# Weight sums for a seven-product output projection: made earlier, in place, in buffers that are idle until the operands come

## The chip, the cores and the metric

One core of a Trainium2 chip runs the kernel. The metric is the time of one execution on the device, in microseconds. The kernel before takes 945.11 us (median of three runs, 944.76 to 945.55).

## What is computed

Sliding-window attention (window 64) is followed by two gated layers. With 4 x 576 = 2304 tokens:

```python
x = attention(q, k, v)                                   # (2304, 512)
x = (sigmoid(x @ w_gate) * (x @ w_val)) @ w_out          # inner width 1536
y = ((x @ w_a) * (x @ w_b)) @ w_out2                     # inner width 1536
```

The inputs q, k and v are float32, and the weights come as 64-bit words, which the kernel decodes into a high and a low float32 part on VectorE, ScalarE and GpSimd. Every product is taken as three matmuls (high x high, high x low, low x high) in the reduced-width float32 form of TensorE.

## The kernel before, in words

Tokens are in nine blocks of 256. Blocks 0 to 4 are the front, in groups (0), (1, 2), (3, 4). Blocks 5 to 8 are the back, whose attention is made meanwhile and parked in DRAM. The inner width is cut into 12 chunks of 128 per layer; chunks F = 0 to 11 are layer 1, and 12 to 23 layer 2.

*The ordered list.* The first ten turns of the plan, with the attention of the front, are an order written out by hand (`RAMP`, with `in_order()` behind it).

*The later turns.* Turns n = 10 to 18 follow: (0) with three chunks, (1, 2) x 3, (3, 4) x 3, (0) x 3, (1, 2) x 2, (3, 4) x 1, (3, 4) x 2, (1, 2) x 2, (0) x 2. A turn makes the gate and value products of its chunks (`hidden`, matmuls `gps` and `vps`, line 450), and the projection that it leaves in the queue is run in the next turn (`accm`, line 551, added into `gacc` on VectorE, line 528). Between the matmuls the loop calls a step of the weight decoder once or twice per block. In turns 10 to 13 (`SPAN`) it also moves the attention of the back along (scores `sps`, transposes `tps`, output `xps`). From turn 14 on the attention's buffers are closed, and pools for later work are opened in their place (`late`: `op6`, `hs`, `wq`, `sts`, `rs`).

*Who sets the order.* Behind the ordered list a planner in the framework places each instruction in the queue of its engine, by program order and by a simulated timeline; on the chip each engine runs its queue in order. A tile that reuses another one's buffer is planned behind all accesses of that other one, also behind those that come later in the program. `held_back(step)` ties what the step issues, in the planner's order alone, behind the newest TensorE instruction of the program (line 844). The chip knows no wait for that.

*The weight sums.* Chunks 0 to 9 of layer 1 are projected once more for the back, in five pairs (p = 0 to 4), by a seven-product scheme for 2 x 2 blocks (`seven`, line 949). It needs four sums of output-weight blocks per pair. `weight_sums(p)` (line 315) makes them in turns 14 to 18, and what is left behind turn 18. It loads the decoded weights from DRAM (for chunks under 7 as a high and a low part that GpSimd adds, line 329), makes four sums of 128x256 on GpSimd (line 338), splits each into high and low on ScalarE and VectorE (lines 340 and 341), and stores all to DRAM (`kept_sums`, line 343). A step makes all of the arithmetic of a pair at once, and the loop calls a step per block, unless layer-2 sums are under way (`combined_by`). Its buffers are from the `late` pools: `hs`, `rs`, `sts`, and `op6`, which has one buffer.

*The operands.* Behind turn 17, `front_operands` (line 715) begins to build the seven operands of the front's layer 2 from the results `b11, b21, b12, b22` (`gacc`). `high(nm, f)` copies f on ScalarE into the high half (line 730), `low(nm)` makes the low half on VectorE (line 736), and `minus(a, b)` puts a - b into b's place on VectorE (line 739). Operands 1 and 5 are placed in four quarters of a buffer set that nothing has used until then, and 6 is placed in `op6`:

```python
o = tuple(quarter(nm // 5, k, f"op{nm}") for k in range(2))     # op1: quarters (0, 0), (0, 1); op5: (1, 0), (1, 1)
for nm, f in ((1, b11), (2, b21)): high(nm, f); low(nm)
yield got                                                       # here turn 18 is put into the program
minus(b12, b11); high(5, b11); low(5); minus(b22, b12); minus(b22, b11); high(6, b11); low(6)
```

The layer-2 products of the front (`quad`, matmuls `qa`, `qb`, `qc` of line 861) use the operands in the order 1, 5, 6, 2, 7, 4, 3.

Of the kernel before, what the change touches and what calls it, by code (L numbers as in the profile page):

```python
# [10 lines left out]
F32 = mybir.dt.float32  # L11
F32R = mybir.dt.float32r
I32 = mybir.dt.int32
U32 = mybir.dt.uint32
AF = mybir.ActivationFunctionType
ALU = mybir.AluOpType
# [5 lines left out]
def tile_window_attention_gated_mlps(ctx, tc, q, k, v, w1g, w1v, w1o, w2a, w2b, w2o, out):  # L22
    nc = tc.nc
    B, H, S, D = q.shape
    NT, DM = out.shape
    DFF = w1g.shape[1]
    P = 128
# [7 lines left out]
    W = 2 * N  # L35
    CH = 2 * P
# [41 lines left out]
    for e in range(2):  # L78
        rows = slice(e * WIN, (e + 1) * WIN)
        nc.gpsimd.affine_select(  # L80
            out=mask_n[rows], in_=mask_n[rows], pattern=[[1, P]], compare_op=ALU.is_ge,
# [3 lines left out]
            out=mask_n[rows], in_=mask_n[rows], pattern=[[-1, P]], compare_op=ALU.is_ge,  # L85
# [159 lines left out]
    x, done = {}, set()  # L245
# [15 lines left out]
    def quarter(i, j, nm):  # L261
        return xs.tile([P, 2, W], F32R, tag=f"q{i}{j}", name=f"{nm}{i}{j}")
# [51 lines left out]

    def weight_sums(p):

        both = late["hs"].tile([P, 2, DM], F32R, tag="hs", name="of").bitcast(F32)
        lows = {}
        for i in range(2):
            F = 2 * p + i  # L320
            if F < DECODED:
                lows[i] = late["rs"].tile([P, W], F32, tag="r", name="ol")
                for j, t in enumerate((both[:, i], lows[i])):
                    nc.sync.dma_start(out=t, in_=kept[F, "o"][:, j])
            else:
                nc.sync.dma_start(out=both[:, i], in_=kept_o[F])
        yield
        for i, low in lows.items():
            nc.gpsimd.tensor_tensor(out=both[:, i], in0=both[:, i], in1=low, op=ALU.add)
        (a11, a21), (a12, a22) = ((both[:, i, 0:CH], both[:, i, CH:]) for i in range(2))  # L330
        u, v = (late["sts"].tile([P, CH], F32, tag="s", name="osum") for _ in range(2))
        o = late["op6"].tile([P, 4, 2, CH], F32R, tag="op6", name="opair")
        for todo in (
            ((u, a21, a22, ALU.add, 0), (v, a11, a21, ALU.subtract, 2)),
            ((u, u, a11, ALU.subtract, 1), (v, a12, u, ALU.subtract, 3)),
        ):
            for s, x, y, op, _ in todo:
                nc.gpsimd.tensor_tensor(out=s, in0=x, in1=y, op=op)
            for s, _, _, _, n in todo:
                nc.scalar.activation(out=o[:, n, 0], in_=s, func=AF.Copy)  # L340
                nc.vector.tensor_tensor(out=o[:, n, 1], in0=s, in1=o[:, n, 0].bitcast(F32), op=ALU.subtract)
        yield
        nc.sync.dma_start(out=kept_sums[p], in_=o.bitcast(F32))

    def load_matrix(F, nm):
        ph, fc = divmod(F, NF)
# [281 lines left out]
    begun, combined_by = [0], []  # L628
# [37 lines left out]
    def step_sums():  # L666

        if summing and 2 * summing[0][0] + 1 in ready and next(summing[0][1], summing) is summing:
            summing.pop(0)
            step_sums()  # L670
# [34 lines left out]
    late = {}  # L705
# [138 lines left out]
    def held_back(step):  # L844

        made = nc.cur_bb.bb.instructions
        since = len(made)
        at = next(i.name for i in reversed(made) if i.engine == mybir.EngineType.PE)
        step()
        for i in nc.cur_bb.bb.instructions[since:]:  # L850
            for after in (at, *copied[-1:]):
                tc.add_manual_dep(
                    i, after, mybir.DependencyInfo(mybir.DependencyClass.NoSync, mybir.DependencyReason.DATA), reason="held"
                )
# [94 lines left out]
    def seven(res, begin, o, sums, b):  # L949


        half = lambda w, i: tuple(p[:, i * CH:(i + 1) * CH] for p in w)
        at = lambda i: tuple(sums[i // 2][:, i % 2, p] for p in range(2))
        a = {1: half(o[0], 0), 2: half(o[1], 0), 3: at(3), 4: half(o[1], 1), 5: at(0), 6: at(1), 7: at(2)}
        jobs = []
        for c in range(2):
            sl, bank, written = slice(c * P, (c + 1) * P), {}, set()

            def job(n, k, start, dsts, bank=bank, sl=sl, c=c, written=written):
                if k not in bank:  # L960
                    bank[k] = ps_acc.tile([P, W], F32, tag="acc", name=f"acc{k}")
                for m, (i, j) in enumerate(((0, 0), (0, 1), (1, 0))):
                    nc.tensor.matmul(  # L963
                        bank[k], lhsT=a[n][i][:, sl], rhs=b[n][j], start=start and m == 0, stop=m == 2,
                        skip_group_check=True,
                    )
                for d in dsts:
                    dst = res[d][:, c]
                    if begin and d not in written:
                        nc.scalar.activation(out=dst, in_=bank[k], func=AF.Copy)  # L970
                    else:
                        nc.vector.tensor_tensor(out=dst, in0=bank[k], in1=dst, op=ALU.add)
                    written.add(d)

            for args in (
                (1, "x", True, (0,)), (2, "y", True, (0,)), (6, "x", False, (1,)), (5, "y", True, (3,)),
                (7, "x", False, (2, 3)), (3, "y", False, (1,)), (4, "y", True, (2,)),
            ):
                jobs.append(lambda args=args, job=job: job(*args))
        return jobs  # L980
# [99 lines left out]
    for n, (group, fcs) in enumerate(plan):  # L1080
        begin, end = fcs[0] == 0, fcs[-1] == NF - 1
        if n < len(FIRST):
            continue
        if n == SPAN.start:
            attend(FRONT[-1][-1])
            feed = attention_stream(BACK[BEHIND:])
        if n == SPAN.stop:
            attend(BACK[-1])
            attend(steps=100)
            next_part(early, (("op6", 1), ("hs", 1), ("wq", 8), ("sts", 4), ("rs", 3)), middle)  # L1090
            limit[0] = NF + 1
        hs = []
        for i, fc in enumerate(fcs):
            need(fc, n)
            hs.append((ready[fc], hidden(0, ready[fc], x[0, group])))
            for _ in range(-(-len(queue) // (len(fcs) - i))):
                queue.pop(0)()
            for _ in group:
                for _ in range(2 if late else 1):
                    step_decode(n)  # L1100
                if late and not combined_by:
                    step_sums()
                if n in SPAN:
                    due += STEPS / ticks
                    attend(steps=int(due))
                    due -= int(due)
        queue.append(lambda a=(group_of[group[0]], group, hs, begin, end): [(m(), e()) for m, e in first_projection(*a)])
        if n == len(plan) - 2:
            built = front_operands(FRONT[2], FRONT[1])
            x_ops = next(built)  # L1110
# [305 lines left out]
```

## Time and profile before

| what | value |
|---|---|
| the time shown: median of three runs | 945.11 us |
| the profiled execution: its time | 945.28 us |
| the profiled execution: first to last instruction | 943.5 us |
| TensorE busy | 922.2 us, 98% |
| VectorE busy | 706.6 us, 75% |
| ScalarE busy | 482.2 us, 51% |
| GpSimd busy | 306.9 us, 33% |

The profile is of one execution. PE is TensorE's matmuls, DVE is VectorE, ACT is ScalarE, POOL is GpSimd, and SP issues the DMAs. Matmuls are pipelined, so a busy PE is not a PE at its peak; what counts here is the time in which PE has no matmul at all, and who released it then.

### The profile page before, as it was taken

How to read it: one execution, taken by the hardware profiler on the slowest of the kernel's cores; microseconds unless marked ns; L12 is line 12 of the kernel's file. 1: busy time of each engine (PE TensorE's matmuls, PEld its weight loads, DVE VectorE, ACT ScalarE, POOL GpSimd, SP SyncE). 2: the span in 40 equal slices, each digit the busy share in tenths (PEclk: the TensorE clock that was granted, in tenths of full speed). 3: DMA queues.
4: the chain of work that ended last, by engine and by line, in shares of the span. 5: the costliest groups of instructions: out<-in, count | busy, mean ns of one | idle time of the engine just before them, and what ended most of it. 6: DMA issues, size and time to landing. Idle time of an engine off the chain costs nothing. (4 is left out here: it accounts for less than half of the span.)

```text
span 943.5 us, 15633 instructions
## 1 busy us (share of the span) xinstructions
PE 922.2 (98%) x5498; PEld 771.9 (82%) x5498; DVE 706.6 (75%) x1370; ACT 482.2 (51%) x1071; POOL 306.9 (33%) x325
## 2 busy tenths in 40 slices
PE   7899999999999999999999999999999999999998
PEld 6798888887888778878787787888888888888886
DVE  6997787786569799898999877687877773354455
ACT  7897555686644456664555446555444233211111
POOL 4543222343226714561655337354351000000000
PEclk9999999999999999999999999999999999999999
DMA  9988598988479626673767758555547675544212
GB/s 225 244 214 239 198 323 290 346 274 250 143 226 315 233 113 200 237 247 142 267 223 250 278 175 234 197 182 168 176 124 240 197 277 147 167 157 146 86 60 89
DMA packets 145566, 195.79 MB, mean 208 GB/s; under 512 B 63569, under 2 KB 98641, under 8 KB 144849
## 3 DMA queue, kind: packets, MB, share of 16 engines
q1 hardware_dynamic: 144400, 192.71, 63.0%
q0 software_dynamic: 1088, 2.10, 1.3%
q8 instruction: 43, 0.70, 0.3%
q14 instruction: 35, 0.28, 0.1%
HBM read 118.75 MB, written 71.57 MB: 202 GB/s over the span
## 5 line engine op out<-in xcount | busy, mean ns | idle before, releaser
L861 PE MATMUL qa<-op,wq 128*128 128x512 f32 x432 | 112.3, 390 | 1.8 <-ACT r L880 1.4
L861 PE MATMUL qb<-op,wq 128*128 128x512 f32 x432 | 111.1, 390 | 0.9 <-POOL wq L430 0.6
L880 ACT ACTIVATE r<-qa 128x512 f32<-128x512 f32 x108 | 62.9, 595 | 95.0 <-PE qa L861 93.4
L450 PE MATMUL gps<-xh,wa 128*128 128x256 f32 (+1 forms) x392 | 104.9, 338 | 1.1 <-DVE g L884 1.1
L450 PE MATMUL vps<-xh,wb 128*128 128x256 f32 (+1 forms) x392 | 105.4, 337 | 0.0
L861 PEld LDWEIGHTS qa<-op,wq 128*128 128x128 f32 x432 | 80.8, 188 | 19.4 <-ACT r L880 2.0
L861 PEld LDWEIGHTS qb<-op,wq 128*128 128x128 f32 x432 | 80.9, 188 | 18.5 <-POOL wq L430 1.0
L551 PE MATMUL accm<-hh,wo 128*128 128x512 f32 (+1 forms) x296 | 85.4, 356 | 1.2 <-DVE gacc L528 1.0
L386 POOL TENSOR_TENSOR wi<-wi,low 128x512 int32<-128x512 int32 x36 | 50.0, 1388 | 112.2 <-DVE wi L382 70.4
L450 PEld LDWEIGHTS gps<-xh,wa 128*128 128x128 f32 x392 | 68.7, 189 | 10.1 <-DVE g L884 1.7
L450 PEld LDWEIGHTS vps<-xh,wb 128*128 128x128 f32 x392 | 68.9, 189 | 7.8 <-issue 0.3
L1000 PE MATMUL accq<-wo,h 128*128 128x512 f32 (+1 forms) x294 | 71.5, 385 | 0.1
L459 ACT ACTIVATE hh<-qa 128x512 fp32r<-128x512 f32 x36 | 21.5, 597 | 91.1 <-DVE qa L894 57.8
L450 PE MATMUL gps<-xl,wa 128*128 128x256 f32 (+1 forms) x196 | 65.6, 335 | 0.6 <-DVE xl L237 0.6
L450 PE MATMUL vps<-xl,wb 128*128 128x256 f32 (+1 forms) x196 | 65.7, 335 | 0.0
L392 DVE SCALAR_TENSOR_TENSOR ex<-ex,wi 128x512 f32<-128x512 f32 x72 | 53.6, 744 | 14.8 <-ACT ex L376 7.0
L1000 PEld LDWEIGHTS accq<-wo,h 128*128 128x128 f32 x294 | 54.5, 188 | 11.3 <-DVE res L1004 0.3
L841 POOL TENSOR_TENSOR wq<-s,wq 128x256 fp32r<-128x256 f32 x48 | 38.4, 865 | 76.2 <-ACT wq L838 76.2
L551 PEld LDWEIGHTS accm<-hh,wo 128*128 128x128 f32 x296 | 52.9, 189 | 11.1 <-DVE gacc L528 3.1
L1000 PE MATMUL accq<-wo,hh 128*128 128x512 f32 x184 | 55.7, 394 | 2.9 <-ACT hh L459 1.9
L189 ACT ACTIVATE pr<-pr,stat 128x128 f32<-128x128 f32 x144 | 54.1, 392 | 7.1 <-DVE stat L183 7.0
L861 PE MATMUL qa<-op,wa 128*128 128x512 f32 x216 | 56.6, 390 | 0.6 <-ACT wb L398 0.6
(187 smaller groups left out, 2178.3 us busy)
## 6 DMA issues: line engine op xcount, KB each, us to landing
wo<-ko SPq DMA_DIRECT2D x27, 512.0 KB, 4.1
wa<-ka SPq DMA_DIRECT2D x27, 512.0 KB, 4.3
st_o<-in_moe_w_out_dram SPq DMA_DIRECT2D x24, 512.0 KB, 4.8
ka<-wa SPq DMA_DIRECT2D x24, 512.0 KB, 5.1
kb<-wb SPq DMA_DIRECT2D x24, 512.0 KB, 4.2
ko<-wo SPq DMA_DIRECT2D x24, 512.0 KB, 5.0
kq<-wq SPq DMA_DIRECT2D x48, 256.0 KB, 4.8
wq<-kq SPq DMA_DIRECT2D x48, 256.0 KB, 3.2
```

The lines of the kernel that those rows point to most:

```text
L189: nc.scalar.activation(out=pr[e][:, j, :], in_=pr[e][:, j, :], func=AF.Exp, bias=nmax[:, e, j:j + 1], scale=-1.0, accum_out=None if t in O ...
L386: (nc.vector if F >= NF else nc.gpsimd).tensor_tensor(out=wi, in0=wi, in1=low, op=ALU.add)
L392: nc.vector.scalar_tensor_tensor(out=wf, in0=wf, scalar=SMALLEST, in1=wi.bitcast(F32), op0=ALU.is_ge, op1=ALU.mult)
L450: nc.tensor.matmul(ps, lhsT=a[:, c * P:(c + 1) * P], rhs=b[:, c, :], start=(n == 0), stop=(n == 3 * NP - 1))
L459: nc.scalar.activation(out=hh, in_=hr, func=AF.Copy, scale=factor)
L551: nc.tensor.matmul(ps[:, m], lhsT=a[:, sl], rhs=b, start=k == 0, stop=k == total - 1)
L841: nc.gpsimd.tensor_tensor(out=t[:, 1], in0=sums[nm], in1=t[:, 0].bitcast(F32), op=ALU.subtract)
L861: nc.tensor.matmul(ps, lhsT=a[:, c * P:(c + 1) * P], rhs=b[:, c, :], start=first and n == 0, stop=n == 5, skip_group_check=True,)
L880: nc.scalar.activation(out=r[n], in_=ps, func=AF.Copy)
L1000: nc.tensor.matmul(ps, lhsT=a, rhs=b, start=n == 0, stop=n == len(pairs) - 1)
```

## The change

`weight_sums` takes its buffers from the quarters of operands 1 and 5 instead of the `late` pools: `pair` is quarter (p % 2, 0), `lows` is quarter (p % 2, 1), and the high parts go into quarter (p % 2, 1) again when the low weights have been added. The low and high weights of a pair are added in one instruction of 128x1024 (of 128x512 for p = 3; p = 4 has none). The four sums are made in place, each in the block of a term that is no longer needed, so their order in memory becomes 6, 7, 3, 5 (`seven` reads them so). The split takes two ScalarE and two VectorE instructions of 128x512 per pair instead of four and four of 128x256. Two stores of 512 KB with runs of 1 KB take the place of one store of 1 MB. The generator has a step for each of these parts (six, or five for p = 4, and the store in the step that also loads the next pair). The loop calls it once per block from turn 11 on, through `held_back`, whether or not layer-2 sums are under way.

```diff
     def weight_sums(p):
 
-        both = late["hs"].tile([P, 2, DM], F32R, tag="hs", name="of").bitcast(F32)
-        lows = {}
+        pair, lows = (quarter(p % 2, j, nm) for j, nm in enumerate(("of", "ol")))
+        both, lows = pair.bitcast(F32), lows.bitcast(F32)
+        split = 0
         for i in range(2):
             F = 2 * p + i
             if F < DECODED:
-                lows[i] = late["rs"].tile([P, W], F32, tag="r", name="ol")
-                for j, t in enumerate((both[:, i], lows[i])):
-                    nc.sync.dma_start(out=t, in_=kept[F, "o"][:, j])
+                split = i + 1
+                for j, t in enumerate((both, lows)):
+                    nc.sync.dma_start(out=t[:, i], in_=kept[F, "o"][:, j])
             else:
                 nc.sync.dma_start(out=both[:, i], in_=kept_o[F])
         yield
-        for i, low in lows.items():
-            nc.gpsimd.tensor_tensor(out=both[:, i], in0=both[:, i], in1=low, op=ALU.add)
+        if split:
+            nc.gpsimd.tensor_tensor(out=both[:, 0:split], in0=both[:, 0:split], in1=lows[:, 0:split], op=ALU.add)
+            yield
         (a11, a21), (a12, a22) = ((both[:, i, 0:CH], both[:, i, CH:]) for i in range(2))
-        u, v = (late["sts"].tile([P, CH], F32, tag="s", name="osum") for _ in range(2))
-        o = late["op6"].tile([P, 4, 2, CH], F32R, tag="op6", name="opair")
-        for todo in (
-            ((u, a21, a22, ALU.add, 0), (v, a11, a21, ALU.subtract, 2)),
-            ((u, u, a11, ALU.subtract, 1), (v, a12, u, ALU.subtract, 3)),
+        for dst, x, y, op in (
+            (a22, a21, a22, ALU.add), (a21, a11, a21, ALU.subtract),
+            (a11, a22, a11, ALU.subtract), (a12, a12, a11, ALU.subtract),
         ):
-            for s, x, y, op, _ in todo:
-                nc.gpsimd.tensor_tensor(out=s, in0=x, in1=y, op=op)
-            for s, _, _, _, n in todo:
-                nc.scalar.activation(out=o[:, n, 0], in_=s, func=AF.Copy)
-                nc.vector.tensor_tensor(out=o[:, n, 1], in0=s, in1=o[:, n, 0].bitcast(F32), op=ALU.subtract)
-        yield
-        nc.sync.dma_start(out=kept_sums[p], in_=o.bitcast(F32))
+            nc.gpsimd.tensor_tensor(out=dst, in0=x, in1=y, op=op)
+        yield
+        high = quarter(p % 2, 1, "oh")
+        for i in range(2):
+            nc.scalar.activation(out=high[:, i], in_=both[:, i], func=AF.Copy)
+            yield
+            nc.vector.tensor_tensor(out=pair[:, i], in0=both[:, i], in1=high[:, i].bitcast(F32), op=ALU.subtract)
+        yield
+        for n, t in enumerate((high, pair)):
+            nc.sync.dma_start(
+                out=kept_sums[p][:, :, n], in_=t.bitcast(F32).rearrange("p i (k f) -> p (i k) f", k=2)
+            )
...
-        a = {1: half(o[0], 0), 2: half(o[1], 0), 3: at(3), 4: half(o[1], 1), 5: at(0), 6: at(1), 7: at(2)}
+        a = {1: half(o[0], 0), 2: half(o[1], 0), 3: at(2), 4: half(o[1], 1), 5: at(3), 6: at(0), 7: at(1)}
...
                     step_decode(n)
-                if late and not combined_by:
-                    step_sums()
+                if n >= SPAN.start + 1:
+                    held_back(step_sums)
```

## Rows read from the trace of the kernel before

**Rows 1.** The profile page: busy us of each engine, share of the span.
```profile
PE 922.2 (98%) x5498; PEld 771.9 (82%) x5498; DVE 706.6 (75%) x1370; ACT 482.2 (51%) x1071; POOL 306.9 (33%) x325
```

**Rows 2.** Busy us by stretch: stretch, length, PE, PEld, DVE, ACT, POOL, clock, DMA, GB/s.
```profile
186.00:272.00 86.00, 85.24 (x757) 72.08 (x757) 60.53 (x178) 59.76 (x163) 26.51 (x22) 1.00 0.75 233
272.00:345.00 73.00, 71.77 (x350) 59.22 (x349) 57.77 (x85) 32.97 (x67) 42.90 (x45) 1.00 0.68 240
345.00:362.00 17.00, 16.19 (x101) 14.00 (x100) 16.60 (x25) 9.34 (x16) 0.00 (x0) 1.00 0.18 50
362.00:600.00 238.00, 231.77 (x1089) 191.55 (x1088) 207.94 (x300) 134.54 (x260) 120.79 (x124) 1.00 0.69 232
```

**Rows 3.** PE's waits: 186 to 272 us (first line), 272 to 362 (three).
```profile
PE xps L228 <- ACT pt L118: 0.8, 1, 0.8
...
PE accm L551 <- DVE gacc L528: 1.0, 3, 0.5
PE qa L861 <- ACT r L880: 0.5, 1, 0.5
PE qa L861 <- ACT op L730: 0.3, 1, 0.3
```

**Rows 4.** Groups by line, 272 to 345 us: count, busy us, mean ns, idle before.
```profile
L341 DVE TENSOR_TENSOR opair<-osum,opair 128x256 fp32r<-128x256 f32 x20 | 11.4, 586 | 3.3 <-ACT opair L340 3.0 <-POOL s L422 0.2
L329 POOL TENSOR_TENSOR of<-of,ol 128x512 f32<-128x512 f32 x7 | 9.8, 1418 | 21.7 <-DMA ol<-ko 15.4 <-DMA of<-ko 6.3
L338 POOL TENSOR_TENSOR osum<-of 128x256 f32<-128x256 f32 x10 | 8.6, 871 | 3.6 <-DMA of<-fo 3.4
L340 ACT ACTIVATE opair<-osum 128x256 fp32r<-128x256 f32 x20 | 8.0, 414 | 11.5 <-POOL osum L338 7.9 <-DMA ks<-opair 3.6
```

**Rows 5.** VectorE by shape, 284 to 312 us (first line), 200 to 240 (second).
```profile
L401 DVE TENSOR_TENSOR wb<-ex,wb 128x512 fp32r<-128x512 f32 x2 | 3.0, 1502 | 0.0
...
L401 DVE TENSOR_TENSOR wb<-ex,wb 128x512 fp32r<-128x512 f32 x2 | 1.4, 688 | 0.0
```

**Rows 6.** ScalarE in time: start, us, instruction, idle before it.
```profile
263.71 0.63 ACT L398 ACTIVATE wo<-ex 128x512 fp32r<-128x512 f32 x1 [0.29 <-PE accm L551]
328.36 1.05 ACT L730 ACTIVATE op<-gacc 128x1024 fp32r<-128x1024 f32 x1
340.58 1.06 ACT L730 ACTIVATE op<-gacc 128x1024 fp32r<-128x1024 f32 x1 [0.89 <-DVE gacc L739]
344.50 0.37 ACT L459 ACTIVATE hh<-vps 128x256 fp32r<-128x256 f32 x1
```

**Rows 7.** VectorE in time.
```profile
339.32 1.22 DVE L739 TENSOR_TENSOR gacc<-gacc,gacc 128x1024 f32<-128x1024 f32 x1
341.68 1.23 DVE L736 TENSOR_TENSOR op<-gacc,op 128x1024 fp32r<-128x1024 f32 x1 [0.19 <-ACT op L730]
```

**Rows 8.** PE in time, turn 18 and the first layer-2 products.
```profile
341.22 0.39 PE L551 MATMUL accm<-hh,wo 128*128 128x512 f32 x1
341.80 1.55 PE L861 MATMUL qa<-op,wa 128*128 128x512 f32 x6
344.55 0.28 PE L551 MATMUL accm<-hh,wo 128*128 128x256 f32 x1
344.66 0.28 PE L551 MATMUL accm<-hl,wo 128*128 128x256 f32 x1
...
349.53 0.28 PE L551 MATMUL accm<-hh,wo 128*128 128x256 f32 x1
```

**Rows 9.** The stores of the sums: count, KB each, median us to landing.
```profile
ks<-opair SPq DMA_DIRECT2D x5, 1024.0 KB, 4.4
```

**Rows 10.** SP's own waits, 186 to 345 us: total, times, longest.
```profile
SPq L343 <- DVE opair L341: 11.4, 4, 8.8
SPq L324 <- POOL osum L338: 6.1, 3, 3.3
```

## The prediction

> **What bounds the kernel now.** I read the page first: PE is busy for 98% of the span, and no other engine for more than 75% [rows 1]. The change leaves PE's matmuls as they are, so it can only move time in which PE stands still. Next I cut the span into stretches with the busy time of each engine. The timeline of PE gave the borders: 186 to 272 us is turns 11 to 13, 272 to 345 is turns 14 to 18 with the beginning of layer 2, and 345 to 362 is the building of its operands. PE's idle time is length less busy time: 0.76, 1.23, 0.81 and, from 362 to 600 us, 6.23 us [rows 2]. That is about 9 us in all, just under 1% of the kernel, and more than that is not to be had here. Then I asked for PE's waits in these stretches. In the late turns PE waited three times, 1.0 us in all, for VectorE to empty a bank of the projection (`gacc`), and 0.8 us in three waits at the first layer-2 products. In the turns with attention it waited once, 0.8 us, for ScalarE's copy of the transposed probabilities [rows 3]. Last I read the groups of the sums in the late turns [rows 4], and what stands around the first operands on ScalarE, VectorE and PE [rows 6 to 8].
>
> **What moves, counted by calls.** A sum has six pauses (five for p = 4), and its last call also loads the next pair, so the five need 1 + 6 + 6 + 6 + 6 + 5 = 30 calls. The loop gives one per block and chunk: 6, 6 and 3 in turns 11 to 13, then 4, 2, 4, 4 and 2. The first 15 calls carry p = 0 and 1 whole and p = 2 up to its four sums. The split of p = 2, and p = 3 and 4, stay in turns 14 to 18. So it is about half of the work that leaves the late turns. Call 29 is the last of turn 17, and call 30, the store of p = 4, falls in turn 18.
>
> **Late turns, what is removed.** VectorE loses 8 of its 20 splits there: 8/20 of 11.4 us, 4.6 us of the 57.8 us that it is busy in 73. GpSimd loses six of seven adds (6 x 1.42 = 8.5 us) and twelve of twenty sums (12 x 0.87 = 10.4 us), 18.9 of its 42.9 us [rows 2, 4]. Their ping-pong goes as well: before, ScalarE stood in front of a split for 11.5 us in all, 7.9 us of it for GpSimd's sum [rows 4], with the tanh and the copies of the turn queued behind. GpSimd's part counts twice, since VectorE is slower beside it: the same 128x512 subtraction takes 1.50 us on the mean between 284 and 312 us, and 0.69 us between 200 and 240 [rows 5]. PE's waits for `gacc` are a VectorE that comes late by a few tenths. I take the whole idle time of this stretch as gone, -1.2 us. The bounds: 0, since half of the work stays, and -2.0 (with the 0.81 us of the next stretch).
>
> The Trainium skill (SBUF — State Buffer, section Who interferes with whom) says that a VectorE instruction with two inputs in SBUF and a GpSimd instruction that reads SBUF take turns at one read interface, and that the later one waits for the whole of the other. The trace agrees as far as 1.50 against 0.69 us goes. By that rule the fusing of two adds into one of 128x1024 is no saving but a longer lock, now set among the attention's steps; what that would cost is the third rival.
>
> **Turns 11 to 13, what is added.** The same 18.9 us on GpSimd, which has 26.5 of 86 us there, so it has the room. ScalarE gets four copies of 128x512, 4 x 0.63 = 2.5 us [rows 6], on 59.8, and VectorE four of 0.69 us [rows 5], 2.8 us, on 60.5 [rows 2]. The DMAs are three loads of 1 MB and two stores of 1 MB, 5 MB in 86 us, 58 GB/s beside 233, at a busy share of 0.75 [rows 2]. The loads wait for nothing that is late: a quarter's store lies twelve calls back. Each step has a call's distance from the one before, so the copy seldom waits for GpSimd. Behind the copy stand the attention's `pt` copies, and behind these the `xps` matmuls that waited for 0.8 us already. Nothing is removed here, so the lower bound is 0. For the upper one I use the late turns: five sums went with 1.23 us of idle PE, 0.25 us each, so 0.6 us for two and a half. I take the middle, +0.3 us.
>
> **The stores.** Ten of 512 KB in runs of 1 KB for five of 1 MB, which landed in 4.4 us [rows 9]. Nobody reads them before layer 2 of the front is over, so they cost nothing unless they hold a quarter. On SP's queue the old stores stood in front for 11.4 us until a split was done, and the loads for 6.1 us until the one buffer was free [rows 10]; both go, as the new store comes a call behind its split. The new order of the sums makes the second half of them needed one product earlier (5 now sits with 3); they are fetched a whole pair ahead of use by the queue of seven products, so nothing.
>
> **The first operand.** This is the one new wait. Operand 1 goes into the quarters that p = 4 holds until its store, call 30, which is planned behind the newest matmul of that point: the last one of turn 17's projection, at 341.2 us before [rows 8]. With 0.4 us for the matmul and 4.4 us for the store, the planner cannot have operand 1 ahead of some 346 us; before, its copy ran at 328.4 [rows 6]. On the chip the store needs only its data, which are ready a call earlier, so it has landed by then, and what counts is operand 1's place in ScalarE's queue: behind the last `hh` of turn 18 (344.5 before, with three operand copies ahead of it), so about 343. Queued behind operand 1 are its low half on VectorE, the subtraction in place and the copy of operand 5: 1.05 + 1.23 + 1.22 us [rows 6, 7], so operand 5 begins at 346.5 instead of 340.6, and 6, 7 and 4 follow it. In this time PE has, from 341.7 on, turn 18's projection (24 matmuls, one each 0.11 to 0.12 us, 2.8 us; before, it was strung out from 344.6 to 349.5), six matmuls of operand 2, which has its own place, and six of operand 1 (1.5 us each) [rows 8]: 5.8 us, to 347.5, when operand 5's high half is just there. Layer 2's first products of block group (0) follow. So it is covered with nothing to spare. In return, operand 6 no longer waits for the old last store in its one buffer. Bounds: -0.8 us (all idle of this stretch goes) and +3.0 us (the second rival); I take +0.3.
>
> **362 to 600 us.** PE's order there is planned anew, on a VectorE that is busy for 208 of 238 us [rows 2]. The 6.23 us of idle time will be dealt again. Nothing in the rows gives a sign, so 0, with half of it either way, 3.1 us, as bounds.
>
> **The sum.** -1.2 + 0.3 + 0.3 + 0 = -0.6 us on the profiled 945.28 us (its span of 943.5 and 1.8 around it): 944.7 us. The profiled execution lies 0.17 us above the median shown, which is within the spread of the runs, so I leave it. A difference of 0.2%, 1.9 us, is about the least that can be told from no change.
>
> **Rivals.** First, a gain that carries on: VectorE and SP come out of the late turns ahead, and half of the idle time up to 600 us goes as well: 945.28 - 1.2 + 0.6 - 3.1 = 941.6 us. For it: SP's 17.5 us of waits go, and the decoder of layer 2 hangs on SP's loads. Against it: the decoder is called at fixed points of the program, and a lead of 4.6 us on an 87% busy VectorE is soon used. Second, slower: operand 1 really starts when the store lands, because SP issues it late or the planned order keeps it there. Then it starts at 346.0, operand 5's copy ends at 346.0 + 1.05 + 1.23 + 1.22 + 1.06 = 350.6, and PE, out of other work at 347.5, stands for 3.0 us: 945.28 + 3.0 - 0.6 = 947.7 us. It decides from the point at which the store is issued after 341 us. Third, the lock among the attention's steps: one add of 128x1024 takes 2 x 1.42 = 2.8 us, three of them lie in turns 11 to 13, and if one holds VectorE's softmax chain just ahead of an `xps` that has no slack, PE stands for 2.8 us: 947.5 us. Against it: ample idle time of VectorE (25 of 86 us) and one such wait only. Fourth, that half of the work stays late and nothing moves, 945.3 us; that is inside the forecast's range.
>
> **How the numbers follow.** The forecast, with its own range from 943.2 to 947.0: 0.48. The first rival 0.31, the second 0.13, the third 0.08. So faster 0.31, same 0.48, slower 0.21. The range goes from below the first rival, by one more microsecond, to above the second: 940.5 to 948.5 us, which takes in the half of the idle time either way.
>
> **What would show it.** The idle time of 272 to 345 us near 0 and no wait for `gacc` there show the first step; `xps` waits above 0.8 us in turns 11 to 13 speak for the third rival, and VectorE instructions of 2 us or more beside a GpSimd add. Operand 1's copy at 342 to 344 us, with its store landed long before, is the forecast; a semaphore wait of ScalarE there and idle PE behind 345 us is the second rival. If the time leaves 943 to 947 us while these stretches do as foretold, the dealing anew behind 362 us was wrongly put at 0.

## The result, and the profile after

The changed kernel takes 951.53 us (median of six runs, 950.79 to 956.4) against 945.33 us (six runs, 944.15 to 946.21), so 6.2 us slower. The ratio is 1.0079, interval 1.0056 to 1.0102. Here and below the ratios are near those of the means and not of the medians, and two of the six runs after were longer (954.51 and 956.4 us). The forecast was 944.7 us, with a range that ended at 948.5.

The profiled execution took 956.4 us, the longest of the six. The same kernel was profiled once more in the experiments (e3, 951.66 us); the account further below uses that one. The page after, the row that answers to [rows 1]:

```profile
PE 926.5 (97%) x5498; PEld 776.4 (81%) x5498; DVE 710.5 (74%) x1360; ACT 480.0 (50%) x1061; POOL 312.6 (33%) x322
```

The busy times by stretch after, in the columns of [rows 2]:

```profile
186.00:272.00 86.00, 83.82 (x738) 69.68 (x738) 63.78 (x180) 59.94 (x166) 37.33 (x32) 1.00 0.83 264
272.00:345.00 73.00, 72.69 (x379) 62.30 (x378) 51.57 (x72) 29.48 (x55) 33.84 (x32) 1.00 0.58 205
345.00:362.00 17.00, 15.56 (x91) 13.61 (x90) 14.69 (x19) 7.56 (x12) 0.00 (x0) 1.00 0.01 1
362.00:600.00 238.00, 225.05 (x1037) 185.10 (x1036) 207.97 (x292) 130.40 (x251) 119.75 (x117) 0.98 0.68 223
```

The reader is to see four things. In turns 11 to 13 PE stands for 2.18 us instead of 0.76. In the late turns it stands for 0.31 us instead of 1.23, and VectorE has 6.2 us less to do. Where the operands are built it stands for 1.44 us instead of 0.81. And from 362 to 600 us it stands for 12.95 us instead of 6.23, with a clock of 0.98 on the mean: more than the other three together. PE's waits after, of 186 to 272, 272 to 362 and 362 to 600 us, against [rows 3]:

```profile
PE xps L228 <- ACT pt L118: 2.0, 2, 1.7
...
PE qb L866 <- ACT op L735: 1.4, 1, 1.4
PE accm L556 <- DVE gacc L533: 0.3, 1, 0.3
...
PE accq L1005 <- ACT hh L464: 3.1, 1, 3.1
PE qa L866 <- DVE op L781: 2.9, 1, 2.9
PE qa L866 <- ACT r L885: 2.3, 1, 2.3
PE qa L866 <- DVE g L889: 1.9, 1, 1.9
PE qb L866 <- DVE qc L889: 1.3, 1, 1.3
```

Before, the longest waits of the last stretch, 362 to 600 us, were these:

```profile
PE accq L1000 <- ACT hh L459: 1.9, 2, 1.3
PE gps L450 <- DVE g L884: 1.1, 1, 1.1
PE qa L861 <- ACT r L880: 0.9, 1, 0.9
```

To find where the time goes I compared the moments at which TensorE has the same amount of matmul work behind it in both traces. The difference is called the lag here; what each execution has at 186 us, before the change begins, is taken off. Each entry is us behind the kernel before, at the time that stands above it in the trace of before. From 600 us to the end no lag changes by more than 0.1 us.

| kernel | 205 | 245 | 286 | 328 | 350 | 392 | 434 | 476 | 539 | 600 |
|---|---|---|---|---|---|---|---|---|---|---|
| changed (first trace) | 1.7 | 1.4 | 2.2 | 0.4 | 1.1 | -1.5 | 4.4 | 5.7 | 3.8 | 11.3 |
| e3: changed, again | 1.7 | 1.4 | 2.0 | 0.1 | 0.8 | -1.8 | 3.9 | 6.8 | 4.9 | 6.6 |
| e1: changed, old order | 1.7 | 1.4 | 2.3 | 0.3 | 4.7 | 7.7 | 7.7 | 7.7 | 7.7 | 7.7 |
| e2: before, new order | 0.0 | 0.0 | 0.0 | -0.2 | 5.1 | 2.5 | 8.4 | 9.7 | 7.8 | 9.6 |
| e4: other quarters | 1.7 | 1.4 | 2.1 | 0.1 | -1.6 | 1.3 | 1.4 | -0.4 | 0.2 | 2.0 |
| e5: other quarters, old order | 1.7 | 1.4 | 2.3 | 0.4 | 0.6 | 0.4 | 0.4 | 0.4 | 0.4 | 0.4 |
| e10: late begin, old order | 0.0 | 0.2 | 0.3 | -1.8 | 8.1 | 7.6 | 7.6 | 7.6 | 7.6 | 7.6 |
| e15: early end | 1.7 | 3.0 | 3.5 | 3.2 | 1.5 | 1.3 | 1.3 | 1.3 | 1.2 | 1.2 |
| e16: late begin, early end | 0.0 | 0.2 | 0.3 | 0.4 | -1.4 | -1.4 | -1.4 | -1.4 | -1.4 | -1.4 |

So the changed kernel loses 1.7 us at the first sum and has it back when the late turns are over. At 392 us it is even ahead. Then 5.6 us (5.8 in the first trace) are lost between 412 and 437 us, and some more behind. What stands there? The stretches from 412 to 432 us after, in the columns of [rows 2]; before, PE was idle for 0.9 us in the same stretches, at a clock of 1.00:

```profile
412.00:416.00 4.00, 3.76 (x16) 2.51 (x16) 3.93 (x4) 2.17 (x4) 4.00 (x5) 1.00 0.75 284
416.00:420.00 4.00, 2.68 (x12) 1.91 (x11) 4.00 (x7) 1.71 (x3) 2.03 (x3) 1.00 0.88 280
420.00:424.00 4.00, 2.15 (x10) 1.28 (x8) 3.97 (x6) 2.27 (x5) 4.00 (x5) 1.00 0.92 364
424.00:428.00 4.00, 2.79 (x11) 2.50 (x12) 3.96 (x7) 2.57 (x6) 4.00 (x4) 0.73 0.87 294
428.00:432.00 4.00, 4.00 (x25) 3.77 (x24) 3.80 (x7) 1.48 (x4) 0.19 (x1) 0.84 0.82 272
```

PE is idle for 4.6 us, and VectorE is full: 19.7 of 20 us. Behind PE's idle time the granted clock falls below 1.00 for two rows, which costs another 1.4 us (0.27 of 2.79 plus 0.16 of 4.00). Less the 0.9 us of before, that is 5.1 of the 5.8 us that this trace loses here by the lag. PE's waits here are 1.3 us for `qc`, a combination that VectorE makes, and 3.1 us for `hh`, ScalarE's copy of another one, `qa`. VectorE's timeline shows the queue in which the two stand, start and duration first:

```profile
416.02 1.22 DVE L391 CUSTOM_DVE_ANT_0 wi<-wi,low 128x1024 uint16<-128x1024 uint16 x1
417.16 0.69 DVE L889 TENSOR_TENSOR qc<-qb,r 128x512 f32<-128x512 f32 x1
...
421.98 1.11 DVE L391 CUSTOM_DVE_ANT_0 wi<-wi,low 128x1024 uint16<-128x1024 uint16 x1
423.01 0.69 DVE L899 TENSOR_TENSOR qa<-qa,g 128x512 f32<-128x512 f32 x1
```

Both combinations, `qc<-qb,r` and `qa<-qa,g`, stand behind a decoder step (`wi`), and the copy `hh`, at 424.59 us, behind other steps of ScalarE (`wq`, `ex`). PE runs its queue in order and has nothing ahead of these products to fill the time with: the order has been dealt anew.

### The profile page after: what moved, and what is told of

It is laid out like the page before. It is cut to its first block, busy times and chain, and to the rows that moved or that the text cites. A ratio compares the mean times of both kernels' runs of the same rounds, so it can differ in the third digit from the quotient of the medians.

```text
span 954.6 us, 15613 instructions
## 1 busy us (share of the span) xinstructions
PE 926.5 (97%) x5498; PEld 776.4 (81%) x5498; DVE 710.5 (74%) x1360; ACT 480.0 (50%) x1061; POOL 312.6 (33%) x322
## 4 chain that ended last, share of the span: by engine, by line
PE 73%; DVE 15%; POOL 4%; issue 4%; ACT 3%; DMA 1%; DVEq 0%; POOLq 0%; ACTq 0%
PE qa L866 15%; PE accq L1005 10%; PE gps L455 9%; PE vps L455 8%; PE qb L866 8%; PE accm L556 8%; PE qc L866 4%; PE accy L968 3%; DVE ex L397 2%; PE accx L968 2%; POOL s L427 2%; DVE wi L387 2%; DVE wi L391 1%; PE xps L228 1%; DVE op L781 1%
## 5 line engine op out<-in xcount | busy, mean ns | idle before, releaser
L397 DVE SCALAR_TENSOR_TENSOR ex<-ex,wi 128x512 f32<-128x512 f32 x72 | 59.6, 828 | 15.1 <-ACT ex L381 7.1
L1005 PEld LDWEIGHTS accq<-wo,h 128*128 128x128 f32 x294 | 54.4, 188 | 11.3 <-DVE res L1009 0.3
L866 PE MATMUL qa<-op,wb 128*128 128x512 f32 x216 | 56.4, 397 | 5.1 <-DVE op L781 2.9
L427 POOL TENSOR_TENSOR s<-ex 128x256 f32<-128x256 f32 x24 | 23.4, 976 | 112.0 <-DVE ex L397 112.0
```

What stands on the lines that cost most here:

```text
L397: nc.vector.scalar_tensor_tensor(out=wf, in0=wf, scalar=SMALLEST, in1=wi.bitcast(F32), op0=ALU.is_ge, op1=ALU.mult)
L427: nc.gpsimd.tensor_tensor(out=s, in0=sums[x] if isinstance(x, int) else x, in1=sums[y] if isinstance(y, int) else y, op=op)
L866: nc.tensor.matmul(ps, lhsT=a[:, c * P:(c + 1) * P], rhs=b[:, c, :], start=first and n == 0, stop=n == 5, skip_group_check=True,)
L1005: nc.tensor.matmul(ps, lhsT=a, rhs=b, start=n == 0, stop=n == len(pairs) - 1)
```

## The experiments

Sixteen runs. The question was where a 1% loss comes from that appears 80 us behind the last store of the sums (332.4 us). Theory A: the order of the engines' queues behind turn 18. Theory B: operand 1, which stands in quarters that are free only when the sums are stored. To hold an order, a kernel gets ties in the planner's order alone, between neighbours of the other kernel's planned queue, for the instructions of an engine behind turn 18 (all but the sums' own). The chip knows no wait for them. "Old order" is this edit, with `ranks` from the kernel before:

```diff
+    for engine, ranks in order.items():
+        own = [i for i in instructions[behind:] if i.engine == engine and i.name not in of_sums]
+        for j, n in zip(ranks, ranks[1:]):
+            tc.add_manual_dep(own[n], own[j].name, NoSync, reason="pinned")
```

**e1: the changed kernel, old order.** In e1 and e2 the ties begin behind turn 18's projection and the building of the seven operands (2712 instructions on PE). From e5 on these are tied too (2736 on PE), but for operands 1 and 2, which stand ahead of turn 18 in the program.

> The changed kernel, with the instructions behind turn 18 held on each of the five engines in the order that the planner gave them in the kernel before. Theory A (the loss lies in the new order of the queues behind 400 us, and the early sums cost nothing themselves): the two losses of the changed kernel's profile, 6.5 us near 412 to 430 us and 8.3 us near 580 to 596 us, go, and the time is 943 to 945.5 us, at or up to 2 us under the kernel before, as the changed kernel was 1.3 us ahead at 400 us. Theory B (the early sums, their DMAs or the first operand's wait cost the 6 us, whatever the order): 949 to 952 us.

953.19 us, ratio 1.0072 (1.0058 to 1.0087). Nothing is lost behind 380 us, as theory A has it, but 7.4 us are lost before it. PE's waits from 320 to 385 us:

```profile
PE qa L872 <- ACT op L741: 2.5, 1, 2.5
PE qb L872 <- ACT op L741: 1.8, 1, 1.8
PE qa L872 <- DVE op L747: 0.8, 1, 0.8
PE qb L872 <- DVE op L747: 0.5, 1, 0.5
```

All of them are for operands, 5.6 us in all: `qb` waits for operand 5 and `qa` for operand 6, whose copies stand behind operand 1's (341.59 us). Behind these waits, from 354 to 362 us, the granted clock was 0.66 and 0.50. Theory B is right as well, and the time lies above its range: with the old order of the products the operands come too late. That the new order is the planner's answer to this is still to be shown; e15 does it.

**e2: the kernel before, with the changed kernel's order** (the same edit, ranks the other way round).

> The kernel before, with the instructions behind turn 18 held in the order that the planner gave them in the changed kernel. Theory A: 950 to 953 us, with PE standing for 2 to 3 us near 420 us and again near 580 us. Theory B: 944 to 946.5 us.

956.41 us, ratio 1.0108 (1.0088 to 1.0127). The old sums in the new order show the changed kernel's waits, in the stretch of 320 to 600 us:

```profile
PE accq L1006 <- ACT hh L459: 3.1, 1, 3.1
PE qa L867 <- ACT r L886: 2.3, 1, 2.3
PE accm L551 <- DVE hl L461: 2.2, 1, 2.2
PE qa L867 <- DVE g L890: 1.9, 1, 1.9
PE qb L867 <- DVE qc L890: 1.3, 1, 1.3
```

The lag from 392 to 434 us grows by 5.9 us in e2 and by 5.7 in e3. The order alone does that. The 5 us that e2 has lost by 350 us, and with them its place above theory A's range, are its own: they go with the wait for `hl`, which the changed kernel does not have.

**e3: the changed kernel, once more.**

> The changed kernel as it is, for a second profile beside that of the 956.4 us execution. Theory A: the time is near 951.5 us and the profile shows at least one of the two losses, near 420 and near 585 us, in the same instructions; which of them comes with a lower granted clock differs between executions. Theory B: the difference is spread over the turns from 186 us on, and no single place holds more than 2 us of it.

952.53 us, ratio 1.0073 (1.005 to 1.0096). It shows the same losses but for the last one, from 539 to 600 us: 1.8 us here and 7.5 in the first trace, so that one is partly chance. Its cause is told at the end: one VectorE instruction took 4.65 us in the first trace and 1.24 in e3.

**e4: the sums in the quarters of the other parity.** Operand 1's quarters are then those of p = 3, which is stored five calls earlier; operand 5's are those of p = 4.

```diff
-        pair, lows = (quarter(p % 2, j, nm) for j, nm in enumerate(("of", "ol")))
+        pair, lows = (quarter((p + 1) % 2, j, nm) for j, nm in enumerate(("of", "ol")))
...
-        high = quarter(p % 2, 1, "oh")
+        high = quarter((p + 1) % 2, 1, "oh")
```

> The changed kernel with the two pairs of quarters exchanged, so that the last sum lies in operand 5's quarters and operand 1's are free from call 25 on. The planner orders all of it anew. If the first operand's wait is what costs (theory B's likeliest form), operand 1's copy starts near 332 us instead of 341 us and 2 to 6 us come back: 946 to 949.5 us. Theory A: the wait at 345 to 362 us (1.4 us of PE) may go, and for the rest the order is dealt once more, so anything from 942 to 953 us, with the difference from the kernel before lying behind 400 us.

947.29 us, ratio 1.0029 (1.0009 to 1.0048): most of the loss goes. At 350 us the kernel is 1.6 us ahead, then 2.9 us are lost by 392 us, 2.4 of them in one new wait, of `gps` for VectorE's `xl` at the first layer-2 products of a block group. The order is still another one than before.

**e5: e4 in the old order. e6: e5 with GpSimd's one addition of 128x1024 made as two of 128x512:**

```diff
-            nc.gpsimd.tensor_tensor(out=both[:, 0:split], in0=both[:, 0:split], in1=lows[:, 0:split], op=ALU.add)
+            for i in range(split):
+                nc.gpsimd.tensor_tensor(out=both[:, i], in0=both[:, i], in1=lows[:, i], op=ALU.add)
```

> The sums as in the changed kernel, but in the quarters of the other parity, so that those of operand 1 come free early, and behind turn 18 the order of all five engines' queues held to that of the kernel before. Theory A (the loss is the new order behind turn 18, with operand 1's late start as what called for it): both causes are gone; about 1.6 us ahead at 348 us, level with the kernel before from 380 us on; 943.5 to 945.3 us against 945.3. Theory B (the early sums cost time by themselves, by DMA or by GpSimd in the turns with attention): 946.5 to 948 us, with the lag already there at 272 us.

> As the kernel with the other quarters and the old order, with GpSimd's one addition of 128x1024 made as two of 128x512. Theory (VectorE waits out one GpSimd instruction, so a shorter one is a shorter lock): the VectorE instruction at 202 to 206 us falls from 2.85 us to about 1.5 us, the wait of xps there from 1.7 us to 0.8 us or less, and the lag at 205 us from 1.7 us to under 0.9 us; the total within 0.5 us of the other, since that lag was made good by 328 us. Rival (VectorE waits until a whole back-to-back run of GpSimd instructions is over): the instruction takes 2.5 us or more again, and the lag at 205 us stays at 1.5 to 1.9 us.

e5: 946.01 us, ratio 1.0008 (0.9999 to 1.0016), between the ranges of its two theories; e6: 944.18 us, 0.9996 (0.9986 to 1.0006), 1.8 us under e5 where 0.5 was expected. Between 350 and 600 us both run with the kernel before. e5 also shows what the early sums are worth by themselves: PE is never idle from 272 to 345 us,

```profile
272.00:345.00 73.00, 73.00 (x369) 62.04 (x368) 53.40 (x73) 30.95 (x56) 33.81 (x32) 1.00 0.58 205
```

but the lag of 2.3 us at 286 us takes all of it back. e6 tests the first part of that lag. VectorE at this place in the kernel before:

```profile
202.22 0.69 DVE L392 SCALAR_TENSOR_TENSOR ex<-ex,wi 128x512 f32<-128x512 f32 x1 [1.47 <-POOL wi L386]
```

VectorE and GpSimd at the first addition, in the changed kernel:

```profile
202.27 2.38 POOL L330 TENSOR_TENSOR of<-of,ol 128x1024 f32<-128x1024 f32 x1
...
202.35 2.85 DVE L397 SCALAR_TENSOR_TENSOR ex<-ex,wi 128x512 f32<-128x512 f32 x1 [1.47 <-POOL wi L391]
```

and in e6:

```profile
202.34 2.97 POOL L331 TENSOR_TENSOR of<-of,ol 128x512 f32<-128x512 f32 x2
...
202.42 1.76 DVE L398 SCALAR_TENSOR_TENSOR ex<-ex,wi 128x512 f32<-128x512 f32 x1 [1.47 <-POOL wi L392]
```

The shorter addition holds VectorE for a shorter time: the instruction takes 1.76 us instead of 2.85 (0.69 in the kernel before), and the lag at 205 us falls from 1.7 to 0.6 us. It waits for one addition here and not for both.

**e9: e6 again. e11: e6 with the two additions a call apart.**

> The kernel with the other quarters, the old order behind turn 18 and the addition made as two of 128x512, once more, to tell whether it beats the kernel before: its trace was 0.9 us ahead from 320 us on. If that lead is its own: 944.0 to 944.6 us against 945.3, a ratio of 0.9990 to 0.9996. If it was chance: within 0.3 us of the kernel before.

> As that kernel, with the two additions of 128x512 one call apart instead of back to back. Theory (VectorE waits out one GpSimd instruction of 1.3 to 1.7 us): the same as with two back to back, 943.8 to 944.8 us, a lag at 205 us of 0.4 to 0.8 us. Rival (two back to back still hold VectorE twice): the lag at 205 us falls below 0.3 us, 943.3 to 944.0 us.

e9: 944.85 us, 0.9995 (0.9986 to 1.0004), between what was expected of a lead and of chance; e11: 945.34 us, 0.9991 (0.9982 to 1.0), a time that neither of its theories has. In e9's trace the lead was gone: near 250 us PE waited for 1.8 us for `xps`, where it waited for 0.6 in e6, so how a sum meets the softmax chain changes from one execution to the next. e11 shows the lag of 0.65 us at 205 us again, so two additions back to back are not the trouble. Neither kernel is shown to be faster than the one before.

**e7: e5 with the sums called as before, in turns 14 to 18 and without `held_back`. e8: e4 with the old order held from turn 10 on.**

> The sums in place in quarters of the other parity and the old order behind turn 18, but made in turns 14 to 18 alone, as before. It tells the in-place form from the early start. Theory A: no lag at 205 us, idle PE time in 272 to 345 us of 0.6 to 1.3 us (1.23 before, 0.3 with the early start); operand 1's quarters are taken until the last sums, so up to 2 us late at 350 us; 944.5 to 947 us. Rival (the early start is worth nothing): the same time as the early start in the old order, within 0.5 us.

> As the kernel with the other quarters, with the order of the kernel before held for all instructions but the sums' own from turn 10 on. Theory A: the sums then only fill gaps; 943.5 to 945.5 us, no difference behind 380 us. Rival (the planner had good reason to move other work around the early sums): PE waits in turns 11 to 13, 946 to 949 us, with the lag there at 272 us.

e7: 964.72 us, 1.0205 (1.0192 to 1.0218). It failed as an experiment: with buffers that are idle from the beginning and no tie, the planner put the sums of the first three pairs at 138 to 184 us, and p = 4's behind 537 us. From 545 to 585 us PE has one wait, of 12.2 us, for ScalarE, whose operand copy waits there for a load; I did not follow it further. e8: 947.45 us, 1.0026 (1.0017 to 1.0035), as its rival had it: the old order in turns 11 to 13 gives no help; the lag is 4 us at 245 us, with a clock of 0.75 and 0.82 from 206 to 214 us.

**e10: e6, begun one turn later** (`n >= SPAN.start + 2`). **e12: e6 with the planner's own order.**

> As that kernel, with the sums begun one turn later (from the third turn behind the ordered list on). Theory (each early sum costs where its addition meets the softmax chain, and the late turns give 1.9 us back once, however much of the work has left them): the lag of 0.6 us at 205 us goes, the 1.9 us at 320 us stays, 943.0 to 944.0 us. Rival (the gain in the late turns goes with the amount of work moved): the gain at 320 us falls to 1.2 us or less, 944.5 to 945.5 us.

> The other quarters and the addition as two of 128x512, with the order left to the planner. Theory A (the new order behind turn 18 costs by itself, even with operand 1 early): as with the other quarters and one addition, less the 1 us at 205 to 265 us: 945.8 to 947.0 us, 1.5 to 3 us slower than the same kernel in the old order. Rival (it was the lock's lag that set the cost behind 345 us): 944 to 944.8 us.

e12: 946.69 us, 1.0015 (1.0005 to 1.0024), as its theory A had it: with the order left to the planner the same kernel loses what e4 lost behind 350 us. e10: 953.79 us, 1.0084 (1.007 to 1.0098), against an expected 943 to 944. The lag at 205 us is gone and the gain of the late turns is there (1.8 us ahead at 328 us). But the later begin moves the end: p = 3 is stored in turn 18 and p = 4 behind it, at 345.8 us, so that the quarters are again taken too long, here those of operand 5. Its copy on ScalarE's timeline (346.92 us in the changed kernel, 340.58 before), and PE's waits from 320 to 385 us:

```profile
349.01 2.00 ACT L742 ACTIVATE op<-gacc 128x1024 fp32r<-128x1024 f32 x2 [4.93 <-DMA ks<-of]
...
PE qb L873 <- ACT op L742: 5.4, 1, 5.4
PE qa L873 <- ACT op L742: 2.2, 1, 2.2
```

The wait of 5.4 us is for operand 5, that of 2.2 for operand 1. This miss shows theory B on its own, in quarters of the other parity and for operand 5: the wait on the store is named by the trace, and the lag grows by 9.8 us between 328 and 350 us.

**e13: the changed kernel's quarters, old order, two additions, and two calls for one from turn 14 on. e14: e10 with these two calls.** What was still open, then: whether it is the moment at which the quarters come free, or the form and place of the sums.

```diff
-                if n >= SPAN.start + 1:
+                for _ in range((n >= SPAN.start + 1) + (n >= SPAN.start + 4)):
                     held_back(step_sums)
```

> The quarters of the changed kernel (operand 1 in those of p = 4), the old order behind turn 18, the addition as two of 128x512; the sums begin where the changed kernel begins them, but from turn 14 on they get two calls for each one, so that p = 4 is stored in turn 16 and not in 18. Theory (what costs 7 us in the old order is operand 1 waiting for its quarters, whichever these are): level with the kernel before at 350 to 380 us, 944 to 946 us. Rival (it is these quarters or the in-place form, not the moment at which they come free): late by 5 us or more at 350 us, 950 to 953 us.

> The other quarters, the old order behind turn 18, the addition as two of 128x512; the sums begin one turn later than in the changed kernel, with two calls for each one from turn 14 on. Theory (as the run with the late begin alone: no lag at 205 us and 1.7 to 2.0 us ahead at 320 us, and with operand 1's quarters free in time nothing is lost at 350 us): 943.0 to 944.2 us. Rival (the doubled calls crowd the late turns): the gain at 320 us falls under 0.8 us, 944.5 to 946 us.

e13: 944.85 us, 0.9989 (0.998 to 0.9998); e14: 943.74 us, 0.9992 (0.9978 to 1.0005). Both lose nothing at the operands, with either parity. e14 differs from e10 in the two calls alone. It is the moment of release. One expectation failed: by 320 us e14 has none of the 1.7 to 2.0 us of the late turns, as its rival had it; it wins 1.5 us between 328 and 350 us.

**e15: the changed kernel with that edit alone, the planner free. e16: e14 with the planner free.**

> The changed kernel with one line changed: from turn 14 on the sums get two calls for each one, so that p = 4 is stored in turn 16; one addition of 128x1024, and the planner free to order everything. Theory (the planner turns its order around because it has operand 1 late; with the quarters early it deals again, by other costs): no operand waits at 345 to 380 us, and a loss behind 362 us of 0 to 3 us: 945 to 948.5 us, against 952.5 of the changed kernel. Rival (the new order behind 400 us comes whatever operand 1 does): 950 to 953 us.

> The run with the late begin and the early end, with the order left to the planner. If its new dealing behind turn 18 costs by itself, as with the other quarters: 1.4 to 3 us more than in the old order, 945.2 to 946.8 us. If that cost went with the lag in turns 11 to 13: 943.2 to 944.4 us.

e15: 945.71 us, ratio 0.9999 (0.9987 to 1.001). One line takes the 6 us back. PE's longest waits from 362 to 600 us are again those of the kernel before:

```profile
PE accq L1005 <- ACT hh L464: 1.8, 2, 1.3
PE gps L455 <- DVE g L889: 1.1, 1, 1.1
PE qa L866 <- ACT r L885: 1.0, 1, 1.0
```

The planned queues say why. Of the instructions behind turn 18 (2736 on PE, 647 on VectorE, 486 on ScalarE), those that stand at another place than in the kernel before, the sums' own left out:

```
                    PE   VectorE   ScalarE
changed kernel     781     210       173
e4                 745     183       166
e15                  4       0         0
e16                 25       0         0
```

The traces bear this out: by tiles and shapes alone, which cannot tell all instructions apart, 606, 567, 4 and 20 of PE's stand at another place. With the quarters of both operands free in time the planner finds the old order by itself. Operand 1's alone are not enough: e4 has them early and those of operand 5 late, and keeps a new order, although on the chip operand 5's copy comes hardly later there than before (341.54 us against 340.58). So theory A and B are one chain: the late store, the late operand, the new order, the loss behind 400 us.

e16 joins what the others gave: begun a turn later (no lag at 205 us), ended early, two short additions, the other parity. 942.98 us against 945.52, ratio 0.9974 (0.9966 to 0.9983). It is faster than both kernels, by 0.26% against the one before, and a little under both ranges: the planner's own order costs nothing here. Its stretches:

```profile
186.00:272.00 86.00, 85.18 (x755) 71.60 (x754) 64.33 (x182) 60.75 (x167) 33.37 (x29) 1.00 0.80 252
272.00:345.00 73.00, 71.91 (x358) 60.36 (x357) 54.72 (x75) 31.43 (x57) 37.46 (x39) 1.00 0.64 225
345.00:362.00 17.00, 16.54 (x106) 14.59 (x105) 16.60 (x25) 9.53 (x16) 0.00 (x0) 1.00 0.20 60
362.00:600.00 238.00, 231.86 (x1088) 191.52 (x1087) 207.86 (x299) 134.40 (x260) 121.52 (x125) 1.00 0.69 231
```

PE's idle time is 0.82, 1.09, 0.46 and 6.14 us, against 0.76, 1.23, 0.81 and 6.23 in [rows 2]: a little in each of the last three. That is 0.5 us in all; the lag has 1.4 us by 350 us, and the rest isn't in these rows.

## Why the prediction was wrong

*The late turns* (-1.2 us, bounds 0 and -2.0): right in kind. The lag falls by 1.9 us between 286 and 328 us in the changed kernel, and `gacc` waits shrink from 1.0 to 0.3 us.

*Turns 11 to 13* (+0.3 us, upper bound 0.6): mis-sized. It came to +2.0 us at 286 us. The bound was taken from late turns, where no softmax chain stands between VectorE and PE. What happened is the third rival's mechanism at the first of the additions: VectorE 2.85 us beside one addition of 2.38, the `pt` copy behind it, and `xps` waiting for 1.7 us. The rival had the addition and the wait at 2.8 us and let it decide the sign. It did not, because the late turns gave the 2 us back. By the Trainium skill (SBUF — State Buffer, section Who interferes with whom) the wait is for the whole of the other instruction. The trace agrees at this place (the addition took 2.38 us, and 2.85 less 0.69 is 2.2), and so does e6. At another place it does not, as told at the end.

*The stores* (0): right on the chip. The two of p = 4 were issued at 329.9 and 332.4 us, and no wait names them. What they hold up is the planner's order, which is the step that failed, below.

*The first operand* (+0.3 us, bounds -0.8 and +3.0): right where it looked. The copies of operands 1 and 5 were forecast for 343 and 346.5 us:

```profile
341.18 2.06 ACT L735 ACTIVATE op<-gacc 128x1024 fp32r<-128x1024 f32 x2
...
346.92 1.06 ACT L735 ACTIVATE op<-gacc 128x1024 fp32r<-128x1024 f32 x1
```

PE lost 0.7 us there by the lag, 0.6 by idle time, in one wait of 1.4 us for operand 5's copy, the one that was to be "just there". The second rival, the start at the store's landing, did not occur: the copy did not wait for a store.

*362 to 600 us* (0, with 3.1 us either way): the step that failed. "Nothing in the rows gives a sign, so 0." It came to +5.8 us (0.8 at 350, 6.6 at 600 us in e3), and the prediction had named this as what a time outside 943 to 947 us would mean. It had the sign in its own hands: it had worked out that the planner cannot have operand 1 ahead of some 346 us, against 328.4 before, and used that for the start of operand 1 alone. Here the planner, with the operand 17.6 us later by these figures, dealt 781 of 2736 places on PE anew, and put PE's partners behind other steps, of the decoder above all, in the queues of ScalarE and of a VectorE that is 87% busy. The order it gives up was one in which PE lost 6.2 us in 238. And half of the idle time of before is no bound for what a worse order can lose: a loss isn't limited by what is idle now. By e1, had the order stayed, the late operands would have cost 7.4 us at once: behind the cover "to 347.5 us" PE would have waited 5.6 us for operands 5 and 6. The changed kernel has one wait of 1.4 us of these, because the planner had put other products there.

What stays open: which of the 781 moves cost the 5.6 us at 412 to 437 us, and at what times the planner's own timeline had the operands, which was not kept. That one execution lost 5.7 us more from 539 to 600 us than the other is chance, told at the end.

## What to carry to other kernels

Where a planner orders the queues, a buffer that is shared with something needed later is judged by the moment at which the planner, not the chip, sees it come free; if that moves behind the next user's old start, expect a new order for what is behind it. By the lag from 350 to 600 us that cost 5.8 us here (e3), where VectorE is 87% busy, and 3.6 us in e4. Ask what the smallest edit is that ends the borrowing earlier: here two calls instead of one, from turn 14 on, were worth 6 us. When a loss stands far behind the change, hold the old order and see whether the loss goes or moves to the place that caused it.

## What the runs showed of the hardware that was not expected

A VectorE instruction can wait for more than one GpSimd instruction. VectorE and GpSimd in the first trace of the changed kernel:

```profile
573.13 5.32 DVE L781 TENSOR_TENSOR op<-t,op 128x1024 fp32r<-128x1024 f32 x1
...
573.75 0.92 POOL L839 TENSOR_TENSOR s<-wf 128x256 f32<-128x256 f32 x1
...
575.84 0.91 POOL L839 TENSOR_TENSOR s<-wf 128x256 f32<-128x256 f32 x1
```

The subtraction takes 1.22 us elsewhere [rows 7] and 5.32 here, beside a run of short GpSimd instructions, and it ends only when the run has had a break. It does so in e3 as well, and the kernel before has one of 5.31 us (`t<-xq,t` at 567.65 us). In the first trace a second one followed, but not in e3; the first line is of the first trace, the second of e3:

```profile
582.91 4.65 DVE L781 TENSOR_TENSOR op<-t,op 128x1024 fp32r<-128x1024 f32 x1 [0.52 <-ACT op L780]
...
583.75 1.24 DVE L781 TENSOR_TENSOR op<-t,op 128x1024 fp32r<-128x1024 f32 x1 [0.52 <-ACT op L780]
```

In both a GpSimd instruction of 0.72 us had begun 0.56 to 0.57 us earlier. In the first trace GpSimd's next ones took 0.71 us each and VectorE waited for the whole run; in e3 VectorE went first, and the next one took 1.71 us. PE has a wait of 2.9 us for this operand in the first trace and none in e3, and the clock behind it costs another 2.8 us or so (below): together the 5.7 us by which the two executions differ from 539 to 600 us. In e6, too, VectorE got in between two additions. What decides is not to be seen in these traces.

The granted clock behind a wait of PE: in the first trace it was 0.73 and 0.84 from 424 to 432 us, behind the 4.6 us of idle PE. From 588 us on it was 0.50 for four microseconds, all of them at the lower of the two levels (1.2 GHz), behind a stretch of 4 us with PE busy for 0.88; from 592 to 596 us it was 0.86. In e3 it was 1.00 from 584 to 596 us.

```profile
584.00:588.00 4.00, 0.88 (x2) 0.57 (x3) 4.00 (x2) 0.19 (x1) 2.48 (x4) 0.78 0.52 173
588.00:592.00 4.00, 4.00 (x10) 3.12 (x10) 1.46 (x3) 0.60 (x1) 0.00 (x0) 0.50 0.61 198
```

Behind the wait of 1.7 us for `xps` it stayed at 1.00 in the changed kernel, and in e15, with the same wait, it was 0.82 and 0.75 from 206 to 214 us.
